# A statically planned attention and two-layer FFN kernel: longer assumed transfer times in the planner, and score products in four quarters of the TensorE array

## The chip, the cores and the metric

The kernel runs on one core of one Trainium2 chip. The metric is the device time of one execution in microseconds. Before the change the median of three runs is 1062.91 us (1062.42 to 1064.74).

The engines are named as in the profile: PE is TensorE's matmul, PEld its weight load, DVE VectorE, ACT ScalarE, POOL GpSimd, SP SyncE, which issues most DMAs.

## The reference

For 4 batches of 12 heads, 448 positions and head size 64:

```python
scores = (q @ k.T) / 8
scores = cap * tanh(scores / cap)
attn = exp(scores - max(scores));  attn /= attn.sum() + 1e-9
x = attn @ v                       # heads side by side: 1792 tokens x 768
h = x @ w_in                       # 768 -> 2048
g = where(h >= 1, h, where(h <= -1, 0, (h + 1)**2 / 4))
y = g @ w_out                      # 2048 -> 768
m = maximum(y @ w1, y @ w2, y @ w3)
out = m @ moe2_w_out               # 768 -> 768
```

The kernel takes the weights as 64-bit words and converts them to f32 on the chip.

## The kernel before

**Tiling.** A batch is 448 tokens, held with features on the partitions. Heads go in pairs (6 per batch). For a pair, the scores come in four chunks of 112 keys; one chunk is a *score step*: two f32 products, one per head, written to two PSUM banks (`ps_s`). Head 0 lies on partitions 0 to 63 and head 1 on 64 to 127, so the two products use the upper and the lower half of the array's rows. The trace shows each f32 product as two weight loads and two matmuls (two passes). The sums over keys (`ps_r`, L478) and the products with v (`ps_a`, L571) use the two halves of the array's columns instead.

**Softmax.** ACT takes tanh of `ps_s` (L425); DVE takes the maximum over the chunks (`mx`, L256), POOL reduces it over partitions (`mb`, L446), DVE subtracts it, ACT takes exp (L464). In batches 1 to 3 DVE first adds the four chunks (`se`) and PE sums that once. The sum is copied to `rs` (L516). For most pairs of batches 0 and 1 its reciprocal takes a round trip: ACT issues two small DMAs that gather 8 rows of 112 into `rc` (L532), DVE inverts them (L550), SP stores `rc` to DRAM (L538) and reads it back spread over the partitions (L543). Then DVE forms `xf` = `ps_a` x `rs`, and `x`.

**FFN.** Each f32 factor is split into a high and a low part, and each *layer part* is three matmuls (L619, L620, L621). There are 336 parts per batch. 64 weight units per batch are loaded. In batch 0 a unit comes as 64-bit words into `raw` (L328, three buffers), is converted by DVE (L332), ACT (L339) and DVE (L345) into `wf`, stored to DRAM as f32 (L351), and split into `w` (high part L251 or L253, low part L256 on DVE). Batches 1 to 3 load the stored f32 (L365).

**Order.** Nothing is scheduled on the chip. `Plan` (L21 to L191) is a list scheduler that runs when the program is built: every operation has a cost per engine, dependencies, buffers that it takes and a time at which it is wanted (`want`). `Plan.run` steps through a model of the engines (T is PE, D is DVE, A is ACT, P is POOL, Q is SP's DMA issue, S an engine that only waits) and the order of starts in that model is the order in which the instructions are written out (`emit`). Each engine then works through its own list strictly in that order. A DMA counts as landed 2.0 us after its issue cost (L143). The round trip's gather costs ACT 0.7 and is followed by a pure wait of 2.0 on S (L547, L548). A score step costs PE `SCORE` = 0.845, which also enters the length of a batch (`SPAN`, L286) and so every later `want`. Attention of batch b+1 is planned beside the FFN of batch b; that of batch 0 stands alone at the start.

Of the kernel before, what the change touches and what calls it, by code (L numbers as in the profile page):

```python
# [20 lines left out]
class Plan:  # L21
# [29 lines left out]
    def op(self, cost, fn, want, deps=(), uses=(), takes=(), kind=None):  # L51
        o = Plan.Op()
        o.kind = kind
        o.cost, o.fn, o.want = cost, fn, want
        o.deps, o.takes = [d for d in deps if d is not None], list(takes)
        o.uses = list(dict.fromkeys([*uses, *takes]))
        for b in o.uses:
            b.users += 1
        for b in o.takes:
            self.order[b.pool].append((want, len(self.ops), b))  # L60
        o.n, o.out, o.t0, o.t1, o.e = 0, [], None, None, None
        self.ops.append(o)
        return o

    def run(self):
# [17 lines left out]
        events, t, left, done = [], 0.0, len(self.ops), []  # L83
# [21 lines left out]
        while left:  # L105
            moved = True
            while moved:
                moved = False
                ts = [o for o in ready if o.kind and at[id(o)] <= t + 1e-9 and can_take(o)]
                turn = min(ts, key=first) if ts else None  # L110

                only = dict.fromkeys(free_at, 0.0)
                for o in ready:
                    if len(o.cost) == 1 and at[id(o)] <= t + 1e-9:
                        e = next(iter(o.cost))
                        only[e] += o.cost[e]
                for o in ready:
                    if at[id(o)] > t + 1e-9 or o.kind and o is not turn:
                        continue
                    idle = [e for e in o.cost if free_at[e] <= t + 1e-9]  # L120
                    if not idle:
                        continue
                    e = next(iter(o.cost))
                    if len(o.cost) > 1:
                        ends = {e: max(free_at[e], t) + only[e] + c for e, c in o.cost.items()}
                        e = min(ends, key=ends.get)
                    if e not in idle or not can_take(o):
                        continue
                    for b in o.takes:
                        free[b.pool] -= 1  # L130
                        queue[b.pool].remove(id(b))
                    c = o.cost[e]
                    if o.kind:
                        c += self.TURN if o.kind != last else 0.0
                        last = o.kind
                    if e == "P":
                        free_at["D"] = max(free_at["D"], t) + self.SHARE
                        heapq.heappush(events, (free_at["D"], serial, None))
                        serial += 1
                    if e == "Q":  # L140

                        free_at[e] = t + c
                        o.t0, o.t1 = t, t + c + 2.0  # L143
                    else:
                        free_at[e] = t + c
                        o.t0, o.t1 = t, t + c
                    o.e = e
                    ready.remove(o)
                    done.append(o)
                    heapq.heappush(events, (o.t1, serial, o))  # L150
                    heapq.heappush(events, (free_at[e], serial + 1, None))
                    serial += 2
                    left -= 1
                    moved = True
                    break
            if not left:
                break
            if not events:
                raise RuntimeError("the plan is stuck")
            t = max(t, events[0][0])  # L160
            while events and events[0][0] <= t + 1e-9:
                _, _, o = heapq.heappop(events)
                if o is None:
                    continue
                for b in o.uses:
                    b.users -= 1
                    if not b.users:
                        free[b.pool] += 1
                for x in o.out:
                    x.n -= 1  # L170
                    if not x.n:
                        r = max(
                            d.t1 + (0.0 if d.e in x.cost and len(x.cost) == 1 else self.LATENCY)
                            for d in x.deps
                        )
                        if "Q" in x.cost and x.takes:
                            r = max(r, x.want - self.AHEAD)
                        at[id(x)] = r
                        ready.append(x)
                        serial += 1  # L180
                        heapq.heappush(events, (r, serial, None))
                ready.sort(key=lambda o: key[id(o)])
# [12 lines left out]
def kernel(  # L195
# [15 lines left out]
    nc = tc.nc  # L211

    B, H, _, _, S = qk.shape
    D = 64
    P = 128
    C = v.shape[2]
# [26 lines left out]
    op = plan.op  # L243
# [37 lines left out]


    PAIR0, LEAD0 = 9.0, 14.0
    PART, SCORE, STEP = 0.609, 0.845, 0.755
    n_parts = NP * NF + NF * NM + 4 * NP * NM
    SPAN = n_parts * PART + NP * (NCH * SCORE + 5 * STEP)  # L286

# [101 lines left out]
    def attention(b, i, begin, last):  # L389

        first = b == 0
        small = b < 2 and (b or i < NP - 1)
        gap = 0.0 if first else (last - begin - LEAD0) / 10
        qkt, vt = unit("qk"), buf("v", "v", [C, 2, NCH, D])
        t = [unit("t", rows=C) for _ in range(NCH)]
# [17 lines left out]
        for c in range(NCH):  # L413
            ps = buf("s", "ps_s", [P, 2, 512])

            def score(e, c=c, ps=ps):
                for j in range(2):
                    o = slice(j * D, (j + 1) * D)
                    nc.tensor.matmul(  # L419
                        ps.tile[:C, j, :S], qkt.tile[o, 1, c * C : (c + 1) * C],  # L420
                        qkt.tile[o, 0], start=True, stop=True,
                    )

            def tanh(e, c=c, ps=ps):
                nc.scalar.activation(  # L425
                    out=t[c].tile, in_=ps.tile[:C, :, :S], func=AF.Tanh, scale=qscale[:C]
                )

            s = op({"T": SCORE}, score, begin + c * SCORE, [ql], [qkt], [ps], "rows")
            tanhs.append(op({"A": 0.92}, tanh, begin + c * SCORE + 0.5, [s], [ps], [t[c]]))  # L430

        w = begin + 3 + gap
# [5 lines left out]
        for c in range(2, NCH):  # L438
            m0 = op(
                c_tt(2 * KS),  # L440
                lambda e, c=c: tt(e, mx.tile, mx.tile, t[c].tile, ALU.max),
# [10 lines left out]
        w = begin + 4 + 2 * gap  # L452
        ar = op({"P": 2.95}, reduce, w, [m0], [mx], [mb])
        w = begin + 7.5 + 4 * gap
        exps = []
        for c in range(NCH):
            sub = op(
                c_tt(2 * KS),
                lambda e, c=c: tt(e, t[c].tile, t[c].tile, mb.tile, ALU.subtract),
# [4 lines left out]
                lambda e, c=c: nc.scalar.activation(  # L464
                    out=t[c].tile, in_=t[c].tile, func=AF.Exp, scale=cap_sb[:C]
                ),
# [4 lines left out]
        rs, xf, x = half("rs"), half("xf"), unit("x", F32R)  # L471
# [13 lines left out]
        w = begin + 9 + 6 * gap  # L485
# [9 lines left out]
        else:  # L495
# [6 lines left out]
            for c in range(2, NCH):  # L502
                sm = op(
                    c_tt(2 * KS),
                    lambda e, c=c: tt(e, se.tile, se.tile, t[c].tile, ALU.add),
# [6 lines left out]
        w = begin + 10 + 8.2 * gap  # L512
# [9 lines left out]
        ep = op({"A": 0.45, "D": 0.55}, eps, w, sums, [pr], [rs])  # L522
        recips = []
        if small:


            rc = buf("rc", "rc", [2 * NCH, C])
            back = dram.tile([2 * NCH, C], F32, name=f"rc{b}_{i}")

            def gather(e):  # L530
                for j in range(2):
                    nc.scalar.dma_start(  # L532
                        out=rc.tile[j * NCH : (j + 1) * NCH],
                        in_=rs.tile[j * D : j * D + 1].rearrange("p (c q) -> p c q", q=C),
                    )

            def spread(e):
                nc.sync.dma_start(out=back, in_=rc.tile)  # L538

            def spread2(e):  # L540
                for j in range(2):
                    row = back[j * NCH : (j + 1) * NCH].rearrange("c q -> (c q)")
                    nc.sync.dma_start(  # L543
                        out=rs.tile[j * D : (j + 1) * D], in_=row.partition_broadcast(D)
                    )

            r = op({"A": 0.7}, gather, w + 0.05, [ep], [rs], [rc])  # L547
            r = op({"S": 2.0}, lambda e: None, w + 0.06, [r], [rc, rs])  # L548
            r = op(
                {"D": 0.72}, lambda e: nc.vector.reciprocal(out=rc.tile, in_=rc.tile),  # L550
                w + 0.1, [r], [rc],
            )
            r = op({"Q": 0.1}, spread, w + 0.2, [r], [rc])
            recips.append(op({"Q": 0.7}, spread2, w + 0.3, [r], [rs]))
# [10 lines left out]
        w = begin + 11 + 8 * gap  # L565
# [23 lines left out]
        w = last - 4  # L589
# [215 lines left out]
```

## Time and profile before

| | |
|---|---|
| median of three runs | 1062.91 us |
| the profiled execution's own time | 1065.57 us |
| its span, first to last instruction | 1063.7 us |
| PE busy | 1030.8 us (97%) |
| DVE busy | 816.6 us (77%) |
| ACT busy | 508.6 us (48%) |
| granted TensorE clock, mean | 0.996 |

PE's share of 97% is a mean over three stages: attention of batch 0 up to about 80 us, the FFN of batch 0 with the conversion of the weights and attention of batch 1 up to about 346 us, and the rest, in which PE has no idle time until the last matmul. Matmuls are pipelined: one of 370 ns in the record starts about 203 ns after the one before. What counts for PE is therefore the distance of starts.

### The profile page before, as it was taken

What the parts mean: (1) busy time and instruction counts of PE and PEld (TensorE: products, weight loads), DVE (VectorE), ACT (ScalarE), POOL (GpSimd) and SP (SyncE); (2) the same over time, 40 slices, a digit from 0 to 9 for tenths busy, and PEclk for the clock granted to TensorE, in tenths of its full rate; (3) what the DMA queues carried; (4) which work ended last, traced back from release to release, by engine and by line L of the source; (5) the groups of instructions that cost most, each with busy time, mean ns of one, the idle gap of its engine ahead of it and who ended that gap; (6) DMA issues with size and microseconds to landing.
All of it is one profiled execution on the core that took longest, in us unless ns stands there. A gap on an engine that the chain in (4) does not pass through costs nothing.

```text
span 1063.7 us, 13311 instructions
## 1 busy us (share of the span) xinstructions
PE 1030.8 (97%) x4968; PEld 820.8 (77%) x4968; DVE 816.6 (77%) x1116; ACT 508.6 (48%) x742; POOL 85.8 (8%) x28
## 2 busy tenths in 40 slices
PE   8988999998999999999999999999999999999998
PEld 2327677785877878778778787787787899999997
DVE  6979998898988689767778598877787778655552
ACT  6877996655654568324324286434243234200101
POOL 2221010220110101101101011011011000000000
PEclk9989999999999999999999999999999999999999
DMA  6438787887877432344324532333432343334331
GB/s 160 128 111 250 250 224 252 272 311 240 280 283 253 142 117 68 100 120 135 99 91 126 157 107 68 106 99 115 145 90 75 124 126 94 90 109 142 111 104 53
DMA packets 64529, 157.62 MB, mean 148 GB/s; under 512 B 7504, under 2 KB 23504, under 8 KB 64464
## 3 DMA queue, kind: packets, MB, share of 16 engines
q1 hardware_dynamic: 64144, 156.73, 48.0%
q8 instruction: 39, 0.64, 0.3%
q14 instruction: 26, 0.21, 0.1%
q10 hardware_dynamic: 320, 0.04, 0.0%
HBM read 129.14 MB, written 27.56 MB: 147 GB/s over the span
## 4 chain that ended last, share of the span: by engine, by line
PE 69%; DVE 1%; ACT 0%; issue 0%; DVEq 0%; ACTq 0%
PE ps_m L619 20%; PE ps_m L620 20%; PE ps_m L621 20%; PE ps_s L419 4%; PE ps_a L571 4%; PE ps_r L478 1%; DVE se L256 0%; DVE t L256 0%; DVE top L256 0%; DVE raw L332 0%; DVE w L256 0%; DVE wf L345 0%; ACT o L251 0%; DVEq L256 0%; ACTq L251 0%
## 5 line engine op out<-in xcount | busy, mean ns | idle before, releaser
L256 DVE TENSOR_TENSOR w<-wf,w 128x768 fp32r<-128x768 f32 (+1 forms) x256 | 226.4, 887 | 6.1 <-ACT w L251 2.7
L253 DVE CAST w<-wf 128x768 fp32r<-128x768 f32 (+1 forms) x122 | 62.9, 516 | 133.4 <-PE ps_m L621 131.4
L619 PE MATMUL ps_m<-y,w 128*128 128x448 f32 x432 | 160.0, 370 | 0.0
L621 PE MATMUL ps_m<-y,w 128*128 128x448 f32 x432 | 158.1, 366 | 1.7 <-DVE w L256 1.7
L620 PE MATMUL ps_m<-y,w 128*128 128x448 f32 x432 | 158.2, 366 | 0.9 <-DVE y L256 0.9
L621 PE MATMUL ps_m<-x,w 128*128 128x448 f32 x384 | 141.0, 367 | 6.5 <-DVE w L256 6.5
L446 POOL PARTITION_ALL_REDUCE mb<-mx x24 | 85.6, 3567 | 732.9 <-DVE mx L256 649.0
L621 PE MATMUL ps_m<-g,w 128*128 128x448 f32 x384 | 140.6, 366 | 2.0 <-DVE w L256 2.0
L619 PE MATMUL ps_m<-g,w 128*128 128x448 f32 x384 | 142.1, 370 | 0.0
L619 PE MATMUL ps_m<-x,w 128*128 128x448 f32 x384 | 142.0, 370 | 0.0
L620 PE MATMUL ps_m<-g,w 128*128 128x448 f32 x384 | 140.4, 366 | 0.3 <-DVE g L256 0.3
L620 PE MATMUL ps_m<-x,w 128*128 128x448 f32 x384 | 140.4, 366 | 0.0
L251 ACT ACTIVATE w<-wf 128x768 fp32r<-128x768 f32 (+1 forms) x134 | 101.5, 758 | 73.9 <-PE ps_m L621 41.8
L425 ACT ACTIVATE t<-ps_s,qscale 112x896 f32<-112x896 f32 x96 | 92.4, 1003 | 58.6 <-PE ps_s L419 57.3
L464 ACT ACTIVATE t<-t,cap_sb 112x896 f32<-112x896 f32 x96 | 96.2, 1037 | 25.4 <-DVE t L256 25.2
L256 DVE TENSOR_TENSOR t<-t,mb 112x896 f32<-112x896 f32 x96 | 99.9, 1079 | 6.6 <-POOL mb L446 6.6
L419 PE MATMUL ps_s<-qk 64*112 64x448 f32 x384 | 89.6, 573 | 9.8 <-DMA qk<-in_qk 6.4
L619 PEld LDWEIGHTS ps_m<-y,w 128*128 128x128 f32 x432 | 81.1, 188 | 18.6 <-issue 11.5
L621 PEld LDWEIGHTS ps_m<-y,w 128*128 128x128 f32 x432 | 81.2, 188 | 8.8 <-DVE w L256 2.1
L620 PEld LDWEIGHTS ps_m<-y,w 128*128 128x128 f32 x432 | 81.2, 188 | 7.8 <-DVE y L256 1.6
L619 PEld LDWEIGHTS ps_m<-g,w 128*128 128x128 f32 x384 | 72.1, 188 | 16.3 <-issue 8.2
L619 PEld LDWEIGHTS ps_m<-x,w 128*128 128x128 f32 x384 | 72.1, 188 | 16.1 <-issue 5.4
(58 smaller groups left out, 1439.8 us busy)
## 6 DMA issues: line engine op xcount, KB each, us to landing
wf<-w SPq DMA_DIRECT2D x120, 384.0 KB
wf<-w SPq DMA_DIRECT2D x72, 256.0 KB
w<-wf SPq DMA_DIRECT2D x40, 384.0 KB
raw<-in_w SPq DMA_DIRECT2D x18, 768.0 KB
raw<-in_w_in SPq DMA_DIRECT2D x16, 768.0 KB
raw<-in_w_out SPq DMA_DIRECT2D x24, 512.0 KB
qk<-in_qk SPq DMA_DIRECT2D x48, 224.0 KB
w<-wf SPq DMA_DIRECT2D x24, 256.0 KB
```

Source lines behind the costliest of these rows:

```text
L251: nc.scalar.activation(out=out_, in_=in_, func=AF.Copy)
L253: nc.vector.tensor_copy(out_, in_)
L256: nc.vector.tensor_tensor(out=out_, in0=a, in1=b, op=o)
L419: nc.tensor.matmul(ps.tile[:C, j, :S], qkt.tile[o, 1, c * C : (c + 1) * C], qkt.tile[o, 0], start=True, stop=True,)
L425: nc.scalar.activation(out=t[c].tile, in_=ps.tile[:C, :, :S], func=AF.Tanh, scale=qscale[:C])
L446: nc.gpsimd.partition_all_reduce(out_ap=mb.tile.rearrange("p h s -> p (h s)"), in_ap=mx.tile.rearrange("p h s -> p (h s)"), channels=C, re ...
L464: lambda e, c=c: nc.scalar.activation(out=t[c].tile, in_=t[c].tile, func=AF.Exp, scale=cap_sb[:C]),
L478: nc.tensor.matmul(pr.tile[j * D : (j + 1) * D, :S], ones, src.tile[:, j], start=start, stop=stop,)
L571: nc.tensor.matmul(pa.tile[j * D : (j + 1) * D, :S], vt.tile[:, j, c], t[c].tile[:, j], start=start, stop=stop,)
L619: nc.tensor.matmul(ps.tile[:, :S], wh, a.tile[:, 0], start=start, stop=False)
L620: nc.tensor.matmul(ps.tile[:, :S], wh, a.tile[:, 1], start=False, stop=False)
L621: nc.tensor.matmul(ps.tile[:, :S], wl, a.tile[:, 0], start=False, stop=stop)
```

## The change

It does three things.

- In the planner a DMA counts as landed 3.2 us after its issue cost, not 2.0. The gather of the round trip costs ACT 1.16 in place of 0.7, and the wait behind it is 3.0 in batch 0 and 5.0 in batch 1, in place of 2.0.
- A score step's product of 64 x 112 per head is issued as two products, of 64 and of 48 output rows: the array is used in its four quarters. The output, the moving data and the number of columns that stream are the same. There are four f32 products per step in place of two, in 96 steps.
- `SCORE` is 0.76, so a batch is planned 24 x 0.085 = 2.04 us shorter and the whole plan is computed anew. Line numbers behind the score step grow by 4.

```diff
                     if e == "Q":
                         free_at[e] = t + c
-                        o.t0, o.t1 = t, t + c + 2.0
+                        o.t0, o.t1 = t, t + c + 3.2
...
-    PART, SCORE, STEP = 0.609, 0.845, 0.755
+    PART, SCORE, STEP = 0.609, 0.76, 0.755
...
             def score(e, c=c, ps=ps):
-                for j in range(2):
-                    o = slice(j * D, (j + 1) * D)
-                    nc.tensor.matmul(
-                        ps.tile[:C, j, :S], qkt.tile[o, 1, c * C : (c + 1) * C],
-                        qkt.tile[o, 0], start=True, stop=True,
-                    )
+                for k in (0, D):
+                    n = min(D, C - k)
+                    for j in range(2):
+                        o = slice(j * D, (j + 1) * D)
+                        nc.tensor.matmul(
+                            ps.tile[k : k + n, j, :S],
+                            qkt.tile[o, 1, c * C + k : c * C + k + n], qkt.tile[o, 0],
+                            start=True, stop=True,
+                        )
...
-            r = op({"A": 0.7}, gather, w + 0.05, [ep], [rs], [rc])
-            r = op({"S": 2.0}, lambda e: None, w + 0.06, [r], [rc, rs])
+            r = op({"A": 1.16}, gather, w + 0.05, [ep], [rs], [rc])
+            r = op({"S": 3.0 if first else 5.0}, lambda e: None, w + 0.06, [r], [rc, rs])
```

DVE's list where the third pair of batch 1 inverts its sums (`se` is the sum over chunks, `w` and `wf` are weights, `y` an FFN result), before:

```order
208 L256 TENSOR_TENSOR y<-ps_m,y 128x448
209 L256 TENSOR_TENSOR w<-wf,w 128x512
210 L345 SCALAR_TENSOR_TENSOR wf<-raw 128x512
211 L332 TENSOR_SCALAR raw<-raw 128x512
212 L256 TENSOR_TENSOR w<-wf,w 128x512
213 L345 SCALAR_TENSOR_TENSOR wf<-raw 128x512
214 L550 RECIPROCAL rc<-rc 8x112
```

And DVE's list at the same place, after:

```order
212 L256 TENSOR_TENSOR y<-ps_m,y 128x448
213 L256 TENSOR_TENSOR w<-wf,w 128x512
214 L345 SCALAR_TENSOR_TENSOR wf<-raw 128x512
215 L332 TENSOR_SCALAR raw<-raw 128x512
216 L256 TENSOR_TENSOR w<-wf,w 128x512
217 L345 SCALAR_TENSOR_TENSOR wf<-raw 128x512
218 L256 TENSOR_TENSOR w<-wf,w 128x512
219 L256 TENSOR_TENSOR mx<-t 112x896
220 L253 CAST w<-wf 128x512
221 L332 TENSOR_SCALAR raw<-raw 128x512
222 L256 TENSOR_TENSOR w<-wf,w 128x512
223 L345 SCALAR_TENSOR_TENSOR wf<-raw 128x512
224 L554 RECIPROCAL rc<-rc 8x112
```

Six instructions more now stand ahead of the reciprocal. At the second pair of batch 1 it is eight, at the fourth four, at the fifth three; at the first it is five, at the sixth two.

SP's list around the store of the fourth pair's reciprocals in batch 1 (`rc_3_170`; `qk` is the load of q and k for the pair whose scores come next), before:

```order
121 L351 DMA w_44_142<-wf 128x768
122 L538 DMA rc_3_170<-rc 8x112
123 L328 DMA raw<-in_w 128x768
124 L543 DMA rs<-rc_3_170 64x448 x2
125 L402 DMA qk<-in_qk 64x2x448 x2
```

SP's list at that place, after:

```order
120 L351 DMA w_44_142<-wf 128x768
121 L328 DMA raw<-in_w 128x768
122 L402 DMA qk<-in_qk 64x2x448 x2
123 L542 DMA rc_3_170<-rc 8x112
124 L351 DMA w_45_143<-wf 128x768
125 L328 DMA raw<-in_w 128x768
126 L547 DMA rs<-rc_3_170 64x448 x2
```

The load of q and k and one load of weights moved from behind the store to ahead of it. PE's list keeps the same number of changes between scores, columns and layers: 42 runs of score steps before and after, most of them of two steps.

## Rows read from the trace of the kernel before

**Rows 1.** Stages: length, busy PE, PEld, DVE, ACT, POOL (instructions); clock, DMA share, GB/s
```profile
0.00:78.00 78.00, 66.32 (x294) 22.29 (x296) 61.45 (x68) 60.15 (x69) 20.97 (x10) 0.96 0.46 128
78.00:346.00 268.00, 250.22 (x1191) 196.71 (x1188) 241.75 (x334) 177.13 (x262) 27.94 (x6) 1.00 0.82 262
346.00:1064.00 718.00, 714.23 (x3486) 601.79 (x3484) 513.45 (x716) 271.35 (x411) 36.89 (x12) 1.00 0.36 108
```

**Rows 2.** PE's waits in 78:165, 165:211, 211:253, 253:296, 296:346 in turn
```profile
PE ps_m L621 <- DVE w L256: 6.5, 6, 1.7
...
PE ps_m L621 <- DVE w L256: 1.7, 2, 1.2
...
PE ps_m L621 <- DVE w L256: 2.0, 2, 1.7
PE ps_m L620 <- DVE y L256: 0.9, 1, 0.9
...
PE ps_s L419 <- DMA qk<-in_qk: 2.2, 1, 2.2
...
PE ps_r L478 <- DVE top L256: 1.7, 1, 1.7
```

**Rows 3.** DVE in order of time: the four reciprocals that waited [idle before <-releaser]
```profile
169.94 0.84 DVE L550 RECIPROCAL rc<-rc 8x112 f32<-8x112 f32 x1 [1.27 <-DMA rc<-rs]
...
212.38 0.84 DVE L550 RECIPROCAL rc<-rc 8x112 f32<-8x112 f32 x1 [2.63 <-DMA rc<-rs]
...
253.55 0.84 DVE L550 RECIPROCAL rc<-rc 8x112 f32<-8x112 f32 x1 [3.29 <-DMA rc<-rs]
...
297.08 0.84 DVE L550 RECIPROCAL rc<-rc 8x112 f32<-8x112 f32 x1 [1.96 <-DMA rc<-rs]
```

**Rows 4.** ACT's queue in order of time: the gather of the fourth pair
```profile
247.24 1.22 ACTq L532 DMA_DIRECT2D rc<-rs  x2
```

**Rows 5.** SP's queue in order of time, 247 to 257 us
```profile
247.43 0.43 SPq L351 DMA_DIRECT2D w<-wf  x1
254.41 0.28 SPq L538 DMA_DIRECT2D rc<-rc  x1
...
256.87 1.32 SPq L402 DMA_DIRECT2D qk<-in_qk  x2
```

**Rows 6.** DVE's groups, 78 to 346 us: busy us, mean ns
```profile
L256 DVE TENSOR_TENSOR w<-wf,w 128x768 fp32r<-128x768 f32 x41 | 38.6, 944 | 0.1
...
L332 DVE TENSOR_SCALAR raw<-raw 128x512 int32<-128x512 uint32 x24 | 10.5, 438 | 0.7 <-DMA raw<-in_w_out 0.7
```

**Rows 7.** DVE's waits, 0 to 80 us
```profile
DVE xf L256 <- DMA rs<-rc: 1.9, 2, 1.2
...
DVE rs L559 <- ACT rs L516: 1.7, 1, 1.7
```

**Rows 8.** PE in order of time: a run of two score steps, then the layer
```profile
355.20 1.76 PE L419 MATMUL ps_s<-qk 64*112 64x448 f32 x8
356.89 0.47 PE L619 MATMUL ps_m<-x,w 128*128 128x448 f32 x1
```

**Rows 9.** PEld in order of time: weight loads in rows (355) and in columns (384)
```profile
355.67 0.18 PEld L419 LDWEIGHTS ps_s<-qk 64*112 64x112 f32 x2 [0.20 <-issue]
356.04 0.18 PEld L419 LDWEIGHTS ps_s<-qk 64*112 64x112 f32 x2 [0.20 <-issue]
...
384.52 0.20 PEld L478 LDWEIGHTS ps_r<-se,ones 112*64 112x64 f32 x4 [0.31 <-issue]
384.95 0.14 PEld L571 LDWEIGHTS ps_a<-t,v 112*64 112x64 f32 x2 [0.23 <-issue]
```

**Rows 10.** PEld in order of time: the first score step, whose second head's data came later
```profile
4.15 0.44 PEld L419 LDWEIGHTS ps_s<-qk 64*112 64x112 f32 x2 [4.15 <-DMA qk<-in_qk]
5.03 0.44 PEld L419 LDWEIGHTS ps_s<-qk 64*112 64x112 f32 x3 [0.44 <-DMA qk<-in_qk]
```

**Rows 11.** The page's costliest groups: busy us, mean ns | idle before, releaser
```profile
L425 ACT ACTIVATE t<-ps_s,qscale 112x896 f32<-112x896 f32 x96 | 92.4, 1003 | 58.6 <-PE ps_s L419 57.3
```

## The prediction

> **What bounds the kernel now.** I read the stages first, then the waits of the engine that bounds each stage, then single places in order of time.
>
> The stages [rows 1] show three kernels in one. From 346 us on PE is busy 714.23 of 718.00 us, and the rest is the tail behind its last matmul. Nothing but a shorter sequence on PE can gain there. From 78 to 346 us PE is busy 250.22 of 268.00, so 17.8 us are idle, and DVE is busy 241.75: it converts and splits the weights and does softmax. Up to 78 us neither is full: PE 66.32, DVE 61.45, ACT 60.15.
>
> In the middle stage PE's waits [rows 2] name DVE nearly everywhere: for the low part of a weight (6.5 + 1.7 + 2.0 us), for `y`, for `top`. One is for the load of q and k, 2.2 us. So in that stage DVE is the pacemaker, and what DVE loses is what PE later waits for. DVE's own largest waits there are four of 1.27 to 3.29 us, 9.15 together, for the gathered sums `rc` [rows 3]. The reader is to see that these are reciprocals of 0.84 us standing at the head of DVE's list while a tiny DMA is under way, with ready weight work behind them. The fourth pair shows how it goes on [rows 4, 5]: ACT issues the gather at 247.24, DVE inverts at 253.55, so 6.31 us passed, where the planner allowed 0.7 + 2.0 and some latency. SP's list has the store of the reciprocals next; SP issued a store at 247.43 and then nothing until 254.41, and the load of q and k behind it went out at 256.87. The score step that needed it is PE's wait of 2.2 us.
>
> **Part 1: the longer waits of the round trip.** The change puts 8, 6, 4 and 3 more DVE instructions ahead of the four reciprocals that waited. An instruction there takes between 0.44 us (a conversion step on 512 columns) and 0.94 us (a low part on 768) [rows 6]. Against the waits of 1.27, 2.63, 3.29 and 1.96 us [rows 3] the added work is at least 8 x 0.44 = 3.5, 6 x 0.44 = 2.6, then about 4 x 0.8 = 3.2 and 3 x 0.8 = 2.4, the last two pairs working on 768 columns (0.8 is my estimate between the two rows, nearer to the larger). All four waits are covered but for some tenths: DVE gains about 8.8 of its 9.15 us. No instruction is added; the covered work had to be done anyway and is only done earlier.
>
> What of it reaches PE? Each gain can give back no more than PE waits between that place and the next: after the second pair 1.27 of 1.7; after the third 2.63 of 2.0 + 0.9; after the fourth the load of q and k, 2.2 (it now stands ahead of the store on SP, so this wait goes even if the gather is as late as before); after the fifth 1.7 of 1.7 [rows 2, 3]. Sum 1.27 + 2.63 + 2.2 + 1.7 = 7.8 us. That is an upper value for these places, since a DVE that is no longer late starts to wait for PE, ACT or loads. Below, the bound is nothing. I take 6.5, nearer to the upper end because PE's waits name DVE.
>
> What is late next: the reciprocals themselves come later, and behind each stand the store, the spread and `xf`. For five pairs nobody waits, since their x is needed only in batch 1's FFN. The last pair is moved by two instructions, 2 x 0.94 at most; if nothing covered that it would cost under 2 us, once.
>
> **Part 2: batch 0's round trips and the 3.2 us of every DMA.** In the first 80 us DVE waits 1.9 us for spread reciprocals and 1.7 us for the copy of the last pair's sums [rows 7]. The new list puts `xf` later and starts the last reciprocals behind more weight work. DVE could win 3.6 us; but the order of the whole stage is redrawn, with one cast of x moved from ACT to DVE and more conversion ahead of the last pair. I take 1.5 us gained, with bounds from 3.6 gained to 4 lost (the same size turned round). The longer landing time also shifts loads in batches 1 to 3; there PE waits for nothing [rows 1], so this costs nothing unless it makes a new wait.
>
> **Part 3: quarters.** A run of two score steps takes 356.89 - 355.20 = 1.69 us from its start to the next layer part [rows 8]. It holds four groups of streams, and groups follow each other by 356.04 - 355.67 = 0.37 us [rows 9]. Four times 0.37 is 1.5; the remaining 0.19 is the fill at the start and the change to the layer. So the halves already run at 0.75 us per step inside a run, and 0.845 is that plus half the ends. Quarters stream the same 448 columns in the same two passes, so 0.75 stays, if all four quarters run side by side. What shrinks is the weight load: 112 columns take 0.18 us, 64 columns 0.14. The first group lasts 355.67 - 355.20 = 0.47 in rows and 384.95 - 384.52 = 0.43 in columns [rows 8, 9]. That is 0.04 per run, less some 0.01 for two more starts: 0.03. With 24 runs behind 346 us this is 0.7 us, not the 0.085 x 48 = 4.1 us that the planner's new number has. In the first two stages, where PE has slack, I count nothing.
>
> Can four quarters run side by side? In columns two streams already read the same partitions at once, in rows two read different ones; quarters are both. The doubt is in the order of issue. In the first score step [rows 10] two weight loads, the first head's two passes, stand ahead of the second head's, which waited for its data until 5.03. So each product's two passes stand one behind the other in PE's list. Yet a run of two steps takes four groups and not five: the second head's first pass starts beside the first head's, past the first head's second pass, which cannot have started. PE looks past one held matmul. With quarters it must look past three.
>
> The Trainium skill ("TensorE: Matmul & The Clock Gate", Part 3, "The mechanism") says that matmuls start and end strictly in program order and are not reordered. By that rule a run of two steps would take five groups here, 2.06 us, and the trace has 1.69; so the measurement speaks against the rule for these two-pass products. In quarters the rule would make a step four groups, 1.5 us, and the time that of the last rival below.
>
> **The sum.** 6.5 + 1.5 + 0.7 = 8.7 us. The profiled execution took 1065.57 (span 1063.7 and 1.87 around it), so it would take 1056.9; it lies 2.66 above the median of 1062.91, and against that median the forecast is 1054.2 us.
>
> **The rivals.**
>
> *The gain is given back.* DVE no longer idles at the reciprocals but waits elsewhere (raw loads, ACT's conversion step, POOL), and only what hung on SP remains: 2.2 + 0.7, some 1060 us. For it: DVE is busy 90% of the stage, and its other waits were not removed. Against it: three quarters of PE's waits name DVE's weights, which are ready work.
>
> *The quarters pair up.* PE looks past one held matmul only. Then the second two quarters start with the second pass of the first two. Inside a run nothing is lost, four passes by two per group, but each run ends one group later: 0.375 us. Behind 346 us that is 24 x 0.375 = 9.0, and 18 x 0.375 = 6.8 in the runs before, of which I count half. With parts 1 and 2: 1062.9 - 8.0 + 9.0 + 3.4 = 1067.3, slower than before. It decides as soon as more than about 0.3 us are lost per run behind 346 us. For it: the trace shows looking past one, never past three. Against it: nothing shows a limit either.
>
> *The quarters run two by two throughout.* A step takes 1.5 us. Behind 346 us 48 x 0.75 = 36; in the middle stage 20 x 0.75 = 15; at the start 28 steps become longer than the tanh of 1.00 us that follows each [rows 11], by 0.5 or, with what the two now wait for each other, some 0.45: 28 x 0.45 = 12.6 (an estimate). With the gains: 1062.9 - 8 + 36 + 15 + 12.6 = 1118. Against it: the trace shows neither a shared bus nor a shared bank that would force it; heads write different banks, and the two column halves share one as `ps_r` does now.
>
> *The new order makes a new wait.* One long list is exchanged for another; a stall such as the 2.2 us at 261 us can arise anywhere in the first 346 us. Three to five of these bring 1062 to 1066.
>
> **How the numbers follow.** Forecast 0.62; gain given back 0.15; quarters paired 0.09; two by two 0.07; new waits 0.07. A difference under 0.2% (2.1 us) cannot be told from none here. The forecast is faster, and so is the larger part of the second case: 0.61 + 0.12, together 0.73. The same: the rest of the second and half of the fifth with a little of the first, 0.08. Slower: the third, the fourth and part of the fifth, 0.19. The likeliest case's own range is 1049 to 1061: 5 below if nearly all of PE's wait for DVE goes, 7 above if little does. For eight in ten the range goes from 1047 to 1068, taking in the paired quarters and leaving out the last case of 1118 and some at each end.
>
> **What would show it.** In the profile after: DVE's wait for `rc` in the middle stage near 0 to 2 us in place of 9.1; SP issuing q and k without the pause of 7 us; PE's idle time in that stage near 11 us in place of 17.8; runs of two score steps at 1.66 us behind 346 us, and four weight loads and four matmuls starting within some 30 ns. A first group of two matmuls only, and 2.0 us per run, would be the paired quarters; 3.2 us per run two by two. The forecast is wrong if DVE's waits for `rc` go and PE waits as long as before, or if the first layer part starts later than at 80 us.

## The result, and the profile after

The changed kernel takes 1051.30 us, median of four runs (1049.88 to 1052.29); on the same chip before took 1063.49. The ratio is 0.9876, with a 95% interval of 0.9854 to 0.9898. The forecast was 1054.2, in a range of 1047 to 1068. The profiled execution took 1052.29 us with a span of 1050.5; that of before 1065.57 with 1063.7.

To see in which stage the 13.2 us of span went, I cut both traces at the first layer part of batch 0 and at that of batch 1. The stages of before, cut there (length; busy PE, PEld, DVE, ACT, POOL; clock, DMA share, GB/s):

```profile
0.00:80.02 80.02, 68.34 (x305) 22.86 (x305) 61.73 (x69) 60.79 (x71) 20.97 (x10) 0.96 0.47 134
80.02:352.01 271.99, 254.21 (x1211) 201.58 (x1209) 243.30 (x335) 177.04 (x262) 27.94 (x6) 1.00 0.81 261
352.01:1063.70 711.69, 708.22 (x3457) 596.35 (x3455) 511.61 (x713) 270.80 (x410) 36.89 (x12) 1.00 0.36 107
```

The stages of after:

```profile
0.00:78.02 78.02, 66.49 (x409) 19.89 (x409) 66.12 (x69) 61.85 (x69) 19.99 (x10) 0.98 0.51 139
78.02:339.99 261.97, 253.08 (x1298) 201.11 (x1297) 241.88 (x335) 178.06 (x263) 18.89 (x6) 1.00 0.83 270
339.99:1050.50 710.51, 706.74 (x3649) 592.48 (x3647) 511.67 (x715) 269.62 (x408) 37.05 (x12) 1.00 0.35 107
```

The first stage is 2.0 us shorter, the middle one 10.0, the rest 1.2. In the middle stage PE and DVE do about the same work as before; most of what went is idle time, 17.8 us before and 8.9 after on PE. Of the 2.0 us ahead of it a part may be the clock: in before the granted clock was 0.50 from 69.7 to 76.5 us, in after 0.51 from 72.0 to 75.4 only. At full clock PE would have saved at most half of each, 3.4 and 1.7 us (an estimate), so up to 1.7 of the 2.0.

DVE's longest waits between 78 and 346 us, after (us in total, times, longest):

```profile
DVE w L253 <- PE ps_m L625: 11.2, 7, 4.0
DVE mx L256 <- ACT t L429: 4.0, 3, 2.5
...
DVE raw L332 <- DMA raw<-in_w: 1.2, 1, 1.2
```

The 9.15 us for the gathered sums [rows 3] have no line any more. Instead DVE stands ahead: it waits until PE has used a weight buffer (`w` <- `ps_m`), most of that from 324 us on. The four reciprocals have no idle time ahead of them:

```profile
169.72 0.83 DVE L554 RECIPROCAL rc<-rc 8x112 f32<-8x112 f32 x1
...
207.90 0.83 DVE L554 RECIPROCAL rc<-rc 8x112 f32<-8x112 f32 x1
...
245.64 0.83 DVE L554 RECIPROCAL rc<-rc 8x112 f32<-8x112 f32 x1
...
286.63 0.83 DVE L554 RECIPROCAL rc<-rc 8x112 f32<-8x112 f32 x1
```

For the fourth pair ACT issued the gather at 239.34, so 6.30 us passed here too, as before [rows 4]; only DVE worked meanwhile. SP's queue there:

```profile
241.67 0.33 SPq L328 DMA_DIRECT2D raw<-in_w  x1
242.09 1.32 SPq L402 DMA_DIRECT2D qk<-in_qk  x2
246.50 0.29 SPq L542 DMA_DIRECT2D rc<-rc  x1
```

The load of q and k went out 4.4 us ahead of the store; before it was 2.5 us behind [rows 5]. PE's waits between 78 and 346 us, after:

```profile
PE ps_m L625 <- DVE w L256: 5.4, 4, 2.6
PE ps_r L482 <- DVE top L256: 1.4, 1, 1.4
PE ps_r L482 <- DVE se L256: 1.1, 2, 0.9
PE ps_s L422 <- ACT t L429: 1.0, 1, 1.0
```

The wait for q and k is gone [rows 2]; those for the low parts of weights fell from 10.1 in all to 5.4. One thing was not forecast. ACT converts the upper words of each raw weight (L339) and stood waiting for the loads. ACT's lines for that, before and then after:

```profile
ACT raw L339 <- DMA raw<-in_w_out: 13.1, 11, 2.8
ACT raw L339 <- DMA raw<-in_w: 8.1, 6, 1.8
ACT raw L339 <- DMA raw<-in_w_in: 2.9, 3, 2.2
ACT raw L339 <- DMA raw<-in_w_o: 2.8, 1, 2.8
```

```profile
ACT raw L339 <- DMA raw<-in_w_out: 4.8, 3, 2.3
ACT raw L339 <- DMA raw<-in_w: 3.8, 3, 1.5
```

Together 26.9 us before, 8.6 after. ACT did not idle less for it: from 78 to 346 us it idles 268.00 - 177.13 = 90.9 us before [rows 1] and 87.6 after (180.37 busy). It now waits for weight buffers that PE has to free, before and then after:

```profile
ACT w L251 <- PE ps_m L621: 4.3, 4, 1.5
```

```profile
ACT w L251 <- PE ps_m L625: 20.5, 17, 1.8
```

DVE needs ACT's converted words for its next step (L345) and waited for them hardly at all, before and then after (for ACT as a whole it waited 9.8 and 9.2 us):

```profile
DVE wf L345 <- ACT raw L339: 0.6, 2, 0.4
```

```profile
DVE wf L345 <- ACT raw L339: 0.4, 1, 0.4
```

A run of two score steps, the matmuls of its first 0.03 us alone, and its weight loads, after:

```profile
343.18 1.72 PE L422 MATMUL ps_s<-qk 64*64 64x448 f32 x16
344.83 0.47 PE L623 MATMUL ps_m<-x,w 128*128 128x448 f32 x1
```

```profile
343.18 0.59 PE L422 MATMUL ps_s<-qk 64*64 64x448 f32 x4
```

```profile
343.18 0.20 PEld L422 LDWEIGHTS ps_s<-qk 64*64 64x64 f32 x8 [0.31 <-DMA qk<-in_qk]
343.61 0.14 PEld L422 LDWEIGHTS ps_s<-qk 64*64 64x64 f32 x4 [0.24 <-issue]
343.99 0.14 PEld L422 LDWEIGHTS ps_s<-qk 64*64 64x64 f32 x4 [0.24 <-issue]
```

The run takes 344.83 - 343.18 = 1.65 us, 0.04 less than [rows 8], and matmuls and loads come in groups of four where [rows 9] has two: all four quarters run side by side. The first group lasts 0.43 in place of 0.47.

### The profile page after: what moved, and what is told of

Same layout as the page of the kernel before. It is cut to its first block, busy times and chain, and to the rows that moved or that the text cites. A ratio compares the mean times of both kernels' runs of the same rounds, so it can differ in the third digit from the quotient of the medians.

```text
span 1050.5 us, 14090 instructions
## 1 busy us (share of the span) xinstructions
PE 1026.3 (98%) x5352; PEld 813.5 (77%) x5352; DVE 819.7 (78%) x1118; ACT 509.5 (49%) x740; POOL 75.9 (7%) x28
## 4 chain that ended last, share of the span: by engine, by line
PE 69%; DVE 1%; ACT 0%; issue 0%; DVEq 0%; ACTq 0%
PE ps_m L623 21%; PE ps_m L624 20%; PE ps_m L625 20%; PE ps_s L422 4%; PE ps_a L575 4%; PE ps_r L482 1%; DVE se L256 0%; DVE t L256 0%; DVE top L256 0%; DVE raw L332 0%; DVE wf L345 0%; DVE w L256 0%; ACT o L251 0%; DVEq L256 0%; ACTq L251 0%
## 5 line engine op out<-in xcount | busy, mean ns | idle before, releaser
L450 POOL PARTITION_ALL_REDUCE mb<-mx x24 | 75.7, 3156 | 729.3 <-DVE mx L256 640.4
L468 ACT ACTIVATE t<-t,cap_sb 112x896 f32<-112x896 f32 x96 | 95.9, 1037 | 17.8 <-DVE t L256 17.7
L422 PE MATMUL ps_s<-qk 64*48 64x448 f32 (+1 forms) x768 | 87.8, 564 | 8.4 <-DMA qk<-in_qk 4.4
L623 PEld LDWEIGHTS ps_m<-y,w 128*128 128x128 f32 x432 | 81.1, 188 | 19.1 <-issue 11.3
```

Source lines behind the costliest of these rows:

```text
L422: nc.tensor.matmul(ps.tile[k : k + n, j, :S], qkt.tile[o, 1, c * C + k : c * C + k + n], qkt.tile[o, 0], start=True, stop=True,)
L450: nc.gpsimd.partition_all_reduce(out_ap=mb.tile.rearrange("p h s -> p (h s)"), in_ap=mx.tile.rearrange("p h s -> p (h s)"), channels=C, re ...
L468: lambda e, c=c: nc.scalar.activation(out=t[c].tile, in_=t[c].tile, func=AF.Exp, scale=cap_sb[:C]),
L623: nc.tensor.matmul(ps.tile[:, :S], wh, a.tile[:, 0], start=start, stop=False)
```

## The experiments

The theory was that DVE's waits at the round trip carry most of the gain. Its rivals were the landing time of all DMAs, the quarters, and the luck of a new plan. Each kernel ran beside before; ratios are to before, with 95% intervals. Before's median was 1066.10 us beside the first four kernels, 1064.98 beside the next four and 1065.28 beside the last four. A ratio here is not the quotient of the two medians and differs from it by up to 0.2%; expectations in us are on the scale where before takes 1063.5. Single executions of before took 1061.66 to 1072.28 us, and a profile shows one execution, so a difference of a few us between two profiles need not be one between the kernels.

**Quarters in the old order.** Before, with the new score step alone:

```diff
-                for j in range(2):
+                for k in (0, D):
+                    n = min(D, C - k)
+                    for j in range(2):
...
```

> The kernel before with the quarter products alone; the planner's numbers and so every engine's order stay as before. Theory (the gain is the round trip's wait): a run of two score steps behind 346 us goes from 1.69 to 1.65 us, 24 x 0.04 = 0.9 us, DVE still waits some 9 us for rc in batch 1; 1062.5 us (1061 to 1063.5). Rival (quarters carry the gain, as the planner's 0.76 would have it): 0.085 x 96 = 8 us off, 1055.

1067.71 us, ratio 1.0033 (1.0017 to 1.0048): slower, which neither had (by the medians it is 0.15%). Its first layer part starts at 82.92 us, 2.9 later than before. Behind batch 1's first part its score runs are 0.95 us shorter in all, as after's are, but the distances between its layer matmuls sum to 1.3 us more (610.98 against 609.72), so that stretch takes 708.17 us against 707.86. PE's line at 39 us, and the stage from 40 to 45 us of this kernel and of before:

```profile
39.48 2.31 PE L482 MATMUL ps_r<-t,ones 112*64 112x448 f32 x8 [1.73 <-ACT t L468]
```

```profile
40.00:45.00 5.00, 5.00 (x24) 1.11 (x22) 3.36 (x5) 5.00 (x7) 2.09 (x1) 0.66 0.15 50
```

```profile
40.00:45.00 5.00, 5.00 (x28) 1.63 (x24) 4.00 (x6) 4.14 (x6) 3.17 (x1) 1.00 0.17 46
```

PE waited 1.73 us for an exp, and behind it the granted clock is 0.66 in the mean, against 1.00 in before: part of the stretch ran at the lower of the two levels, 1.2 GHz. That does not account for the 2.9 us, for before ran as long at that level, only later. The stretches at half clock up to the first layer part, in before and then in this kernel:

```profile
69.70:76.50 6.80, 5.25 (x14) 1.72 (x16) 6.62 (x9) 5.42 (x6) 0.00 (x0) 0.50 0.41 111
```

```profile
40.80:44.20 3.40, 3.40 (x14) 0.59 (x12) 2.56 (x4) 3.40 (x5) 1.29 (x1) 0.51 0.20 71
75.00:78.40 3.40, 3.21 (x10) 1.18 (x12) 3.40 (x5) 2.51 (x4) 0.00 (x0) 0.50 0.41 145
```

What PE has more in this kernel is waiting for exps (`ps_r` <- `t`), 6.6 us against 5.0 up to 85 us. The quarters are not the gain. That this order lost time with them in the first stage is seen in one profile; why is not settled.

**The round trip's costs alone.** Before, with

```diff
-            r = op({"A": 0.7}, gather, w + 0.05, [ep], [rs], [rc])
-            r = op({"S": 2.0}, lambda e: None, w + 0.06, [r], [rc, rs])
+            r = op({"A": 1.16}, gather, w + 0.05, [ep], [rs], [rc])
+            r = op({"S": 3.0 if first else 5.0}, lambda e: None, w + 0.06, [r], [rc, rs])
```

> The kernel before with the gather's cost of 1.16 and the waits of 3.0 and 5.0 alone, planned anew; landing time 2.0, score cost and halves as before. Its DVE list has 4, 6, 6, 4, 3 and 2 more instructions ahead of batch 1's six reciprocals, and SP's list has the load of q and k ahead of the fourth pair's store. Theory: most of the gain, DVE's wait for rc in batch 1 under 1 us, 1053.5 us (1051 to 1057). Rival (the 3.2 us landing of all DMAs carries it): 1060 to 1063.

1060.24 us, ratio 0.9956 (0.9932 to 0.9980), which is 1058.8 on the scale of the expectation: a gain, but between the two theories. DVE's wait for `rc` is gone, and PE's for weights fell, but others grew. Its lines of PE and of ACT in the middle stage:

```profile
PE ps_m L621 <- DVE w L256: 4.0, 4, 1.6
PE ps_s L419 <- DMA qk<-in_qk: 3.0, 1, 3.0
```

```profile
ACT raw L339 <- DMA raw<-in_w_out: 15.2, 14, 2.2
ACT raw L339 <- DMA raw<-in_w: 13.2, 9, 2.8
```

ACT's waits for raw loads are 35.8 us in all, more than before's 26.9. They did not reach PE: its idle time fell by 6.4 us, from 17.7 to 11.3, which is about what part 1 had forecast. So this is not the rival "the gain is given back". The 3.0 us for q and k stand at another place than before's 2.2, at 97.7 us; that is a wait which the new order made.

**The landing time alone.** Before, with

```diff
-                        o.t0, o.t1 = t, t + c + 2.0
+                        o.t0, o.t1 = t, t + c + 3.2
```

> The kernel before with the landing time of 3.2 alone, planned anew. Its DVE list has the reciprocals of batch 1 where they were (0, 0, 2, 0, -2 and 0 instructions later). Theory: DVE still waits 7 us or more for rc; 1062 us (1059 to 1066). Rival: 1052 to 1056.

1059.13 us, ratio 0.9940 (0.9920 to 0.9960), 1057.1 on the scale of the expectation. My theory had under 0.4% here; it was wrong to leave this part so small. DVE and ACT in the middle stage:

```profile
DVE rc L550 <- DMA rc<-rs: 7.8, 4, 3.4
```

```profile
ACT raw L339 <- DMA raw<-in_w_out: 11.2, 11, 2.4
ACT raw L339 <- DMA raw<-in_w: 5.4, 5, 1.8
ACT raw L339 <- DMA raw<-in_w_in: 2.9, 2, 1.7
```

So it gains with the wait for `rc` still there, while ACT's waits for raw loads fall to 19.5 us and PE's waits from 17.7 to 12.3.

**The round trip put back in the changed kernel.** After, with the last diff but one reversed.

> The changed kernel with the gather's cost and wait put back to 0.7 and 2.0; landing time 3.2, score cost 0.76 and quarters as after, planned anew. The reciprocals stand where they stood before (0, 2, 0, -1, -2 and -1 instructions later). Theory: the gain goes but for the quarters' 0.9 and the load of q and k, which stays behind the fourth store: 1061 us (1058 to 1066), DVE waits 7 to 12 us for rc. Rival (landing time and score cost carry the gain): 1051 to 1054.

1058.85 us, ratio 0.9928 (0.9904 to 0.9952), 1055.8 on the scale of the expectation: better than expected, as the landing time had been. DVE and PE in the middle stage:

```profile
DVE rc L554 <- DMA rc<-rs: 6.1, 4, 3.6
```

```profile
PE ps_m L625 <- DVE w L256: 8.5, 7, 1.8
```

Both are back, at 6.1 of 9.1 us (7 to 12 were expected) and 8.5 of 10.1. ACT's waits for raw loads stay short, 9.7 us, and yet PE's waits are 13.2.

**The new plan with halves.** After, with before's score step in it.

```diff
-                for k in (0, D):
+                for j in range(2):
...
```

> The changed kernel's plan, the same order on every engine, with each score step as two products in the halves as before. Theory (quarters only shorten the weight load at the start of a run): runs of two steps are 1.69 us again in place of 1.65, 1.5 us slower than the changed kernel in all, 1053 us on the scale where before is 1063.5, ratio to before 0.990. Rival (quarters cost something at the start of the kernel, as the run with quarters in the old order, 0.33% slower, would have it): as fast as the changed kernel or faster, ratio 0.984 to 0.988.

1053.03 us, ratio 0.9883 (0.9858 to 0.9908), beside 0.9876 with quarters. The order makes the gain; the quarters' part, under 0.1%, is below what these intervals can tell.

**The landing time put back in the changed kernel.** After, with 2.0 in place of 3.2.

> The changed kernel planned with the landing time of 2.0 us put back; gather and waits, score cost and quarters as after. Theory now (two gains that mostly add: the round trip's wait about 5 us, the landing time about 6): 0.6% slower than the changed kernel, ratio to before 0.993 to 0.995; DVE's wait for rc near 0, but its waits for rs and raw back. Rival (the wait of the round trip is enough once the score cost is 0.76 too): ratio 0.988.

1054.91 us, ratio 0.9892 (0.9862 to 0.9923): closer to the rival, which had 0.988. Without the landing time the plan loses little when the score cost is 0.76. ACT's longest lines in the middle stage:

```profile
ACT raw L339 <- DMA raw<-in_w: 13.2, 7, 3.5
ACT raw L339 <- DMA raw<-in_w_out: 11.1, 12, 2.1
```

Its waits for raw loads are back at 27.7 us, and most of the gain stays: PE's waits are 11.0 us.

**The landing time split.** Before, with 3.2 for the round trip's own DMAs, and with 3.2 for all others:

```diff
-                        o.t0, o.t1 = t, t + c + 2.0
+                        o.t0, o.t1 = t, t + c + (3.2 if c < 0.75 else 2.0)
```

```diff
-                        o.t0, o.t1 = t, t + c + 2.0
+                        o.t0, o.t1 = t, t + c + (2.0 if c < 0.75 else 3.2)
```

> The kernel before with the landing time of 3.2 us for the round trip's store and spread alone (the DMAs with an issue cost under 0.75), all other DMAs at 2.0. Theory (the landing time gains by putting DVE's xf later, behind the spread's landing): most of what the landing time gives alone, ratio to before 0.994 to 0.996, DVE's wait for rs in the first 80 us under 0.5 us. Rival (it gains by the loads of weights): ratio 0.999 to 1.001.

> The kernel before with the landing time of 3.2 us for all DMAs but the round trip's store and spread. Theory: ratio to before 0.998 to 1.001, DVE still waits some 1.9 us for rs in the first 80 us. Rival (loads of weights carry it): ratio 0.993 to 0.996, ACT's waits for raw loads in the middle stage fall from 27 us.

1064.24 us, ratio 0.9984 (0.9966 to 1.0002), and 1060.46 us, 0.9958 (0.9941 to 0.9975). My theory fell: DVE's wait for `rs` in the first 80 us is gone in the first of the two, as expected, but next to nothing is gained by it. The rival's numbers held, the first all but 0.0006: it is the other DMAs. Which of them (loads of raw weights, stores and loads of converted ones, q and k, v) is not separated. ACT's waits for raw loads are 23.8 us in the first of the two and 19.1 in the second.

**The score cost alone.** Before, with

```diff
-    PART, SCORE, STEP = 0.609, 0.845, 0.755
+    PART, SCORE, STEP = 0.609, 0.76, 0.755
```

> The kernel before with the planner's score cost of 0.76 alone, halves as before, planned anew. A plan 2 us per batch shorter, but nothing in it is nearer to the chip: score steps take 0.845 in runs of two. Theory (only numbers that take waits away gain): ratio to before 0.997 to 1.003, DVE's wait for rc 8 to 10 us. Rival (replanning itself shuffles by half a per cent): 0.993 to 0.996 or over 1.004.

1060.20 us, ratio 0.9952 (0.9933 to 0.9971). This is the rival's number. DVE still waits 8.0 us for `rc` and ACT 28.2 us for raw loads, yet PE's idle time in the middle stage is 13.0 in place of 17.7. I have no mechanism for it: a number that is no nearer to the chip gains half a per cent.

**Round trip and landing time, without score cost and quarters.** After, with 0.845 and halves.

> The kernel before with the round trip's costs and the landing time of 3.2 for all DMAs; score cost 0.845 and halves as before. Theory (these two carry the change, the score cost and the quarters 0.1% at most): ratio to before 0.988 to 0.991, DVE's wait for rc near 0 and ACT's waits for raw loads near 9 us in place of 27. Rival (the score cost has a share): 0.993 or more.

1052.80 us, ratio 0.9880 (0.9861 to 0.9899), as expected: these two alone give what the whole change gives. ACT's waits for raw loads are 18.0 us, not 9, so that part of the expectation missed.

**The wait at 4.0 and at 6.0.** After, with

```diff
-            r = op({"S": 3.0 if first else 5.0}, lambda e: None, w + 0.06, [r], [rc, rs])
+            r = op({"S": 3.0 if first else 4.0}, lambda e: None, w + 0.06, [r], [rc, rs])
```

and the same with 6.0.

> The changed kernel with the wait of batch 1's round trip at 4.0 in place of 5.0. Its DVE list has the six reciprocals 2, 2, 2, 2, 1 and 0 instructions earlier than after. The gathers took 2.2 to 6.3 us. Theory: DVE waits about 1 to 3 us for rc, the time is 0 to 2 us above the changed kernel, ratio to before 0.988 to 0.990. Rival (any new plan scatters by half a per cent): under 0.984 or over 0.992.

> The changed kernel with the wait of batch 1's round trip at 6.0 in place of 5.0; the reciprocals stand 1, -1, 1, 2, 1 and 0 instructions later than after. Theory: nothing is left to gain, DVE waits for rc 0 in both, ratio to before 0.986 to 0.989. Rival as for 4.0.

At 4.0: 1050.52 us, ratio 0.9858 (0.9840 to 0.9877), DVE waiting 1.3 us for `rc`, once. At 6.0: 1048.09 us, ratio 0.9838 (0.9823 to 0.9853), the fastest of all and beyond the changed kernel's own 0.9876. So both expectations missed: at 4.0 nothing was lost, and 6.0 came out at the rival's number, under 0.984. Whether the longer wait or only another order gained is not shown. In the version with 6.0 DVE and PE have in the middle stage:

```profile
DVE w L253 <- PE ps_m L625: 11.4, 7, 3.9
DVE raw L332 <- DMA raw<-in_w: 1.3, 1, 1.3
```

```profile
PE ps_m L625 <- DVE w L256: 3.7, 5, 1.2
PE ps_r L482 <- DVE se L256: 2.1, 4, 0.9
```

PE's waits are 5.8 us there, after has 8.9. A plan around the same waits differs from its neighbour by some 0.2 to 0.4%; that is how much of any single ratio here is the luck of one order.

**All of it in one table.** Ratios to before by the planner's numbers:

| round trip | as before | landing 3.2 | score 0.76 | both |
|---|---|---|---|---|
| 0.7 and 2.0 | 1 | 0.9940 | 0.9952 | 0.9928 (quarters) |
| 1.16, 3.0 and 5.0 | 0.9956 | 0.9880 | 0.9892 (quarters) | 0.9883; 0.9876 (quarters) |

Read down each column, the round trip's costs gain 0.44, 0.60, 0.60 and 0.52%: four pairs of kernels, much the same step, 4.7 to 6.4 us of 1063.5. (Each step is the difference of two ratios that are uncertain by about 0.2% each, so it is itself uncertain by about 0.3%, or 3 us. In the third pair the score step differs too: halves above, quarters below. By the quotients of the medians the four steps are 0.55, 0.52, 0.47 and 0.47%.) Read along the rows, landing time and score cost do not add: whichever comes first gives 0.5 to 0.8%, the one that is added to it 0 to 0.2%.

## Why the prediction was right, and where it was not

**Part 1, the round trip: 6.5 us forecast, 4.7 to 6.4 measured.** Direction, place and mechanism held: the wait for `rc` went to nothing, the load of q and k came out ahead of the store and its wait on PE went, and PE's waits for DVE's weights halved. With the costs put back DVE's wait for `rc` came back at 6.1 us and PE's for weights at 8.5. The sum over the four places with its limit by PE's next wait held as an upper value (7.8).

**Part 2: the failed step.** I wrote that the longer landing time shifts loads "in batches 1 to 3", where it costs nothing, and looked at the first stage for the rest (1.5 forecast; the first layer part came 2.0 us earlier, though behind it two column steps more are still to do). I left out the middle stage, where weights are loaded too. The step that failed is this term, put at nothing because PE waits for nothing later. The landing time alone gave 0.60%, by the other DMAs and not by the round trip's, and PE's waits in the middle stage fell by 5.4 us with it. The middle stage gave 10.0 us in place of 6.5; of the span's 13.2 us that is 3.5 of the 4.5 by which it passed the forecast of 8.7. By which way the landing time acts stays open. ACT's waits for raw loads, 26.9 us before and 8.6 after, look like it, but the other kernels leave little for them. With the round trip's new costs, 8.6 us of them (after), 27.7 (landing time put back) and 35.8 (round trip alone) go with 8.9, 11.0 and 11.3 us of PE's waits. With its old costs, 9.7 (round trip put back), 19.5 (landing time alone) and 28.2 (score cost alone) go with 13.2, 12.3 and 13.0. So some 20 us of ACT's waiting go with 2 us of PE's or with none, and the score cost alone gains as much without shortening them. DVE waited for ACT's conversion 0.6 us in all before and 0.4 after.

**Part 3, quarters: 0.7 us forecast.** 0.04 us for each of 24 runs is 0.96 in the trace, and looking past three held matmuls is shown: loads and matmuls start in groups of four. That the order of starts is not fixed shows at another place too. At the start of after, where the second head's data came late, the first product's second pass starts at 5.25 us, ahead of the second product's first at 5.38; in the runs it starts behind it. From batch 1's first layer part to the last matmul 707.86 us became 706.37; of these 1.49 the runs are about 0.95, a step that every kernel with quarters shows. The other 0.5 lies in the distances between layer matmuls, which sum to between 609.1 and 611.0 us from one kernel to the next, with no cause that I could name; with halves in the new order the stretch is 707.59. On the chip the quarters' part is below the noise. The planner's 0.76 is not what a step now costs (0.825 in a run of two); its gain, where it had one, was another order.

**The rivals.** The two on the quarters fell by the trace. "The gain is given back" fell too, also for the round trip's costs alone: ACT waits 8.9 us longer for raw loads there, but PE's idle time falls by 6.4. The argument against it in the prediction was weaker than it says: DVE's weights have 10.1 of PE's 17.7 us of waits, 57% and not three quarters; all that DVE makes comes to 14.5 us. "A new wait" did not come up in after, but the round trip's costs alone show that it can, with q and k late by 3.0 us at 97.7 us.

**The number.** That 1051.3 lies so near the forecast of 1054.2 is in part luck. Part 1 came out at or under its 6.5 us, and about half of the gain came from where the prediction had counted nothing.

**Open.** Why the score cost alone gains 0.48%, and why the quarters alone lose 0.33%. Both shift nothing that a wait named in the profile would explain; PE's idle time and the granted clock in the first stage differ from plan to plan. One rival was not tested: all five kernels that change one group of the planner's numbers alone came out faster, by 0.16% (not clear of none) to 0.60%, so almost any order drawn anew may beat this one. There is no run with a number that means nothing, or with the score cost moved the other way. For the round trip three of the four pairs compare two new orders, which speaks for it. The landing time's four steps are 0.60, 0.76, 0.24 and 0.16%, so its own worth is not settled.

## What to carry to other kernels

In a kernel whose order is fixed in advance, compare the planner's latencies with the trace's from issue to use: an engine that idles at the head of its list with ready work behind it marks a latency that was taken too short. Read these waits on every engine, but test whether they reach the one that bounds: here some 20 us of ACT's waits for loads went with 2 us of PE's or with none. And when a plan is recomputed, judge a cost by several pairs of plans, not by one: a neighbouring plan can differ by some tenths of a per cent for no reason that the numbers show.

## What was not expected of the hardware

A gather of 8 rows of 112 words took up to 6.2 us from ACT's issue until both halves were there, when the DMA engines were busy 0.82 of the time; the shortest in that stage was 2.2 us.

TensorE started matmuls past three earlier ones that were held for other quarters: a step's first group, four matmuls within 0.02 us at 343.18, holds the first passes of four products whose second passes stand between them in the list, if the list is as the kernel's start has it.

The granted clock fell to half for some microseconds of the first stage at places that differ between profiles. In before it was 0.50 from 69.7 to 76.5 us, and PE stood idle from 67.2 to 71.3. In the kernel with quarters in the old order it was 0.51 from 40.8 to 44.2, behind an idle 1.73 us, and 0.50 from 75.0 to 78.4, and PE stood idle for 4.8 us up to 75.2.
